# An attention-and-experts kernel: f's lead over q, k and v given up, and the last chunk's gate cut into thirds

## The chip, the cores and the metric

The kernel runs on one core of a Trainium2 chip. The metric is device time in microseconds; the median of 3 runs before the change is 465.24 us (465.19 to 465.57). The profile and trace below come from one profiled execution of the same kernel, with a span of 463.4 us and a mean granted TensorE clock of 0.97.

Five engines work in their own order and wait for each other through semaphores: TensorE (PE in the profile; its weight loads are PEld), VectorE (DVE), ScalarE (ACT), GpSimd (POOL) and SyncE (SP), whose queue issues the loads.

## The reference

Two blocks follow one another. The first is a gated linear recurrence over 768 steps for 4 batches and 8 heads of 48 columns; the second sends each of the resulting 3072 rows to one of 8 experts of equal capacity (384 rows).

```python
# attention block: q, k, v, f_logit are (4, 8, 768, 48)
f = 1.0 / (1.0 + np.exp(-f_logit))
for t in range(S):
    state = f[:, :, t, :, None] * state + np.einsum('bhd,bhe->bhde', k[:, :, t], v[:, :, t])
    y[:, :, t] = np.einsum('bhd,bhde->bhe', q[:, :, t], state)
# bridge: x is (3072, 384)
# experts block: w_gate (384, 8), w1 (8, 384, 1024), w2 (8, 1024, 384)
logits = x @ w_gate
order = np.argsort(-logits.flatten())      # best first; each row taken once, 384 rows an expert
...                                        # assigned[row] = expert
for e in range(E):
    mask = assigned == e
    out[mask] = np.maximum(x[mask] @ w1[e], 0.0) @ w2[e]
```

## The kernel before

The recurrence is worked in 24 chunks of 128 time steps (6 along the sequence, 4 batches; chunk i is batch i % 4). Each chunk passes through small functions. A step of the loop calls each of them for a chunk that depends on the function's stage: stage s in step n works on chunk n - s. Each engine takes its instructions in the order in which the functions are called.

```python
def load(G, names):
    b, c = G["b"], G["c"]
    for nm in names:                       # 192 KB each, pieces of 192 bytes
        ...
        nc.sync.dma_start(out=t[:], in_=src[b, :, C * c:C * c + C, :].rearrange("h t d -> t h d"))

def clamp(G):                              # GpSimd, f alone
    nc.gpsimd.tensor_scalar(out=f[:], in0=f[:], scalar1=3.0e38, scalar2=-40.0, ...)
def decays(G):                             # ScalarE, f alone: g = ln(1 + exp(-f))
    nc.scalar.activation(out=f[:], in_=f[:], func=AF.Exp, bias=0.0, scale=-1.0)
    nc.scalar.activation(out=g[:, :, 0:DH], in_=f[:], func=AF.Ln, bias=1.0, scale=1.0)
def split(G):                              # from chunk 2 on: g as high + low
    nc.vector.tensor_scalar(out=upper[:], ...)
    nc.gpsimd.tensor_tensor(out=low[:], in0=g[:, :, 0:DH], in1=upper[:].bitcast(FP32), op=ALU.subtract)
def sums(G):                               # TensorE: running sums L of g (two matmuls, high and low)
    ...
def factors(G):                            # VectorE dl from L, ScalarE eq = exp(-dl), ek = exp(dl)
    ...
def halves(G):                             # TensorE: sums of g over each half chunk ("ends")
    ...
def gated_q(G): ...                        # VectorE:  qg = q * eq
def gated_k(G): ...                        # GpSimd:   kg = k * ek  (VectorE for chunk 0)
def span(G): ...                           # VectorE spans, GpSimd and ScalarE gl: decay of the whole chunk
def columns(G, nm, t):                     # TensorE: transposes T of qg or kg
    if G["i"] in (1, 2):
        idle_turns(4, ps("nothing", "sum"))
    ...
def decayed(G): ...                        # GpSimd: R = state * gl
def added(G): ...                          # TensorE dS = kg' v ("states")
def scores(G): ...                         # TensorE A = kT' qT, VectorE copy_predicated into am
def values(G): ...                         # TensorE Y = am' v
def queries(G): ...                        # TensorE Y += qT' R; ScalarE copies Y to x; x stored to xd

def transposed(G):
    X = ps("X")
    for d in range(DC):                    # DC = 3
        nc.tensor.transpose(out=X[:, 128 * d:128 * d + 128],
                            in_=G["x"][:, 128 * d:128 * d + 128], identity=ident[:])
    G["X"] = X
def x_copy(G, work=work):
    G["xT"] = work.tile([128, DC, 128], FP32, name="xT", tag="xT")
    nc.vector.tensor_copy(out=G["xT"][:].rearrange("p c t -> p (c t)"), in_=G["X"][:, 0:D])
def gate(G):
    X = G["X"]
    for d in range(DC):
        for j in range(2):
            half = slice(HC * j, HC * j + HC)
            nc.tensor.matmul(out=X[half, D:D + E], lhsT=G["xT"][:, d, half], rhs=wg[:, d, :], ...)
def counts_so_far(G):
    if G["i"] == len(chunks) - 1:
        begun[3]()                         # counted(): 20 matmuls, then need = wanted - counts
```

`idle_turns` are matmuls of constants whose result nobody reads; they keep TensorE occupied. f has 3 buffers, q and k 4 each, v 7. The loop, with the orders of a step while the pipe fills, when it is full, and at the end:

```python
FIRST = ((decayed, 2), (q_columns, 2), (k_columns, 2), (transposed, 5), (sums, 0))
FILLING = (FIRST + ((x_copy, 5), (gated_q, 1), (gated_k, 1), (factors, 0), (k_copy, 2),
                    (added, 2), (values, 4), (halves, 0), (gate, 5),
                    (new_state, 2), (decays, -1), (span, 0), (to_logits, 5),
                    (split, -1), (beside, 0), (clamp, -2), (queries, 4), (split_high, -1),
                    (scores, 3)))
FULL = ((decayed, 2), (decays, -1), (transposed, 5), (sums, 0), (added, 2), (x_copy, 5),
        (gated_q, 1), (gated_k, 1), (factors, 0), (split, -1), (split_high, -1), (k_copy, 3),
        (halves, 0), (new_state, 2), (values, 4), (span, 0), (gate, 5), (to_logits, 5),
        (q_columns, 2), (k_columns, 2), (k_last, 2), (beside, 0), (clamp, -2), (queries, 4),
        (scores, 3))
LAST = ((scores, 3),) + FIRST + ((x_copy, 5), (k_copy, 2), (values, 4), (queries, 4),
                                 (counts_so_far, 5), (gate, 5), (to_logits, 5), (beside, 5))

def attention(first, last):
    for step in range(first, last):
        for ahead, names in (AHEAD + 1, "f"), (AHEAD, "qkv"):      # AHEAD = 2
            if AHEAD <= step + ahead < len(chunks) and (ahead == AHEAD or step >= 0):
                load(chunks[step + ahead], names)
        for part, stage in (FILLING if step < STAGES else           # STAGES = 6
                            FULL if step < len(chunks) + 2 else LAST):
            if 0 <= step - stage < len(chunks):
                part(chunks[step - stage])
            ...

for n, names in (0, "f"), (1, "f"), (0, "qk"), (2, "f"), (0, "v"), (1, "qkv"):
    load(chunks[n], names)
nc.sync.dma_start(out=wg[:], ...)
...
idle_turns(19, ps("nothing", "sum"))
clamp(chunks[0])
attention(-1, 2)
idle_turns(12, ps("nothing", "sum"))
attention(2, 3)
nc.vector.memset(a_bufs[2][:], 0.0)        # the third score buffer
```

After the last step come, on VectorE, the best logit of each row of the last column of chunks, its choice, its key, the steps that it reaches (`above`) and the pick; then TensorE counts rows per expert, the first of a search with which the routing begins. The experts' matmuls follow and fill the rest of the span.

Of the kernel before, what the change touches and what calls it, by code (L numbers as in the profile page):

```python
# [26 lines left out]
def kernel(  # L27
# [132 lines left out]
    def load(G, names):  # L160
        b, c = G["b"], G["c"]
        for nm in names:
            src = {"f": f_logit, "q": q, "k": k, "v": v}[nm]
# [35 lines left out]
    def sums(G):  # L199
        g = g_bufs[G["i"] % NB]  # L200
        G["L"] = L = ps("L")
# [136 lines left out]
    def queries(G):  # L338
# [12 lines left out]
        for par in range(2):  # L351
            copy = nc.vector.tensor_copy if par and G["i"] == len(chunks) - 1 else nc.scalar.copy
            copy(out=x[:].rearrange("t (a r d) -> t r a d", r=2, d=DH)[:, par],
                 in_=Y[par][:, 0:HP * DH].rearrange("t (a d) -> t a d", d=DH))
        row = S * b + C * c
        nc.scalar.dma_start(out=xd[row:row + C, :], in_=x[:])

    def transposed(G):
        X = ps("X")
        for d in range(DC):  # L360
            nc.tensor.transpose(out=X[:, 128 * d:128 * d + 128],
                                in_=G["x"][:, 128 * d:128 * d + 128], identity=ident[:])
        G["X"] = X

    def x_copy(G, work=work):
        G["xT"] = work.tile([128, DC, 128], FP32, name="xT", tag="xT")
        nc.vector.tensor_copy(out=G["xT"][:].rearrange("p c t -> p (c t)"), in_=G["X"][:, 0:D])

    def gate(G):
        X = G["X"]  # L370
        for d in range(DC):
            for j in range(2):
                half = slice(HC * j, HC * j + HC)
                nc.tensor.matmul(out=X[half, D:D + E], lhsT=G["xT"][:, d, half], rhs=wg[:, d, :],
                                 start=(d == 0), stop=(d == DC - 1))

    def counts_so_far(G):
        if G["i"] == len(chunks) - 1:
            begun[3]()

    def to_logits(G, to=None):
        if to is None:
            to = logits[:, G["b"] * NCH + G["c"]]
        nc.vector.tensor_copy(out=to, in_=G["X"][:, D:D + E])
# [5 lines left out]
    def beside(G):  # L390
# [9 lines left out]
    FIRST = ((decayed, 2), (q_columns, 2), (k_columns, 2), (transposed, 5), (sums, 0))  # L400
    FILLING = (FIRST + ((x_copy, 5), (gated_q, 1), (gated_k, 1), (factors, 0), (k_copy, 2),
                        (added, 2), (values, 4), (halves, 0), (gate, 5),
                        (new_state, 2), (decays, -1), (span, 0), (to_logits, 5),
                        (split, -1), (beside, 0), (clamp, -2), (queries, 4), (split_high, -1),
                        (scores, 3)))
    FULL = ((decayed, 2), (decays, -1), (transposed, 5), (sums, 0), (added, 2), (x_copy, 5),
            (gated_q, 1), (gated_k, 1), (factors, 0), (split, -1), (split_high, -1), (k_copy, 3),
            (halves, 0), (new_state, 2), (values, 4), (span, 0), (gate, 5), (to_logits, 5),
            (q_columns, 2), (k_columns, 2), (k_last, 2), (beside, 0), (clamp, -2), (queries, 4),
# [923 lines left out]
```

## Time and profile before

| what | value | how to read it |
|---|---|---|
| median time | 465.24 us | 3 runs |
| span of the profiled execution | 463.4 us | 11905 instructions |
| PE busy | 439.1 us (95%) | TensorE; its ends are modelled |
| DVE, ACT, POOL busy | 257.5, 138.8, 131.3 us | 56, 30 and 28% of the span |
| f, q, k, v loads | 24 each of 192 KB | 4.2 to 4.5 us from issue to landing |
| DMA in attention | 160 to 205 GB/s | in the slices up to 116 us |
| experts' matmuls, H and O | 132.6 + 67.0 + 66.7 us | 496 and 491 ns each |
| idle turns, all | 20.2 us | 71 of them |

The page divides the span into 40 slices of 11.6 us. Attention takes about the first fourteen of them: its last logits are copied at 159.54 us. The rest is routing and the experts. The chain that ended last tells little here, since its list holds only the last few microseconds of the queues; the stages have to be read from the timeline instead.

### The profile page before, as it was taken

What the parts mean: (1) busy time and instruction counts of PE and PEld (TensorE: products, weight loads), DVE (VectorE), ACT (ScalarE), POOL (GpSimd) and SP (SyncE); (2) the same over time, 40 slices, a digit from 0 to 9 for tenths busy, and PEclk for the clock granted to TensorE, in tenths of its full rate; (3) what the DMA queues carried; (4) which work ended last, traced back from release to release, by engine and by line L of the source; (5) the groups of instructions that cost most, each with busy time, mean ns of one, the idle gap of its engine ahead of it and who ended that gap; (6) DMA issues with size and microseconds to landing.
All of it is one profiled execution on the core that took longest, in us unless ns stands there. A gap on an engine that the chain in (4) does not pass through costs nothing. (4 is left out here: it accounts for less than half of the span.)

```text
span 463.4 us, 11905 instructions
## 1 busy us (share of the span) xinstructions
PE 439.1 (95%) x4890; PEld 294.6 (64%) x4890; DVE 257.5 (56%) x878; ACT 138.8 (30%) x322; POOL 131.3 (28%) x189
## 2 busy tenths in 40 slices
PE   6898999999998759999999999999999999999994
PEld 3687888888887635565555555555555565556552
DVE  6468777777886677647737737737737737000000
ACT  3556655666552001212212212212212212212210
POOL 2546545555551012023013013013013015201001
PEclk9989999999999857999999999999999999999998
DMA  9999998878511109073072072072072076500001
GB/s 160 180 205 193 202 192 173 177 172 179 124 38 37 54 2 306 18 261 97 18 274 85 18 272 87 18 272 85 19 272 86 17 272 227 202 16 37 0 18 38
DMA packets 118399, 59.11 MB, mean 128 GB/s; under 512 B 101664, under 2 KB 112960, under 8 KB 118336
## 3 DMA queue, kind: packets, MB, share of 16 engines
q1 hardware_dynamic: 111760, 44.06, 38.3%
q0 software_dynamic: 3072, 9.44, 6.2%
q10 hardware_dynamic: 3504, 4.77, 3.0%
q8 instruction: 40, 0.66, 0.6%
q14 instruction: 23, 0.19, 0.1%
HBM read 48.77 MB, written 9.49 MB: 126 GB/s over the span
## 5 line engine op out<-in xcount | busy, mean ns | idle before, releaser
L1054 PE MATMUL H<-xeT,w 128*128 128x384 f32 x384 | 132.6, 496 | 0.1
L1054 PEld LDWEIGHTS H<-xeT,w 128*128 128x128 f32 x384 | 69.1, 190 | 45.7 <-issue 4.0
L1066 PE MATMUL O<-w,hT 128*128 128x384 f32 x192 | 67.0, 491 | 0.0
L1066 PE MATMUL last_O<-w,hT 128*128 128x384 f32 x192 | 66.7, 491 | 0.0
L1058 ACT ACTIVATE hT<-H 128x384 f32<-128x384 f32 x64 | 31.4, 491 | 101.3 <-PE H L1054 85.3
L1066 PEld LDWEIGHTS last_O<-w,hT 128*128 128x128 f32 x192 | 35.1, 190 | 22.8 <-issue 1.9
L1066 PEld LDWEIGHTS O<-w,hT 128*128 128x128 f32 x192 | 34.9, 190 | 21.5 <-issue 1.3
L322 DVE COPY_PREDICATED am<-mask,A 128x512 f32<-128x512 int32 x48 | 32.3, 728 | 26.0 <-PE A L317 26.0
L1071 POOL DMA_INDIRECT out_dram<-o,token x21 | 21.2, 1012 | 83.6 <-ACT o L1070 83.3
L191 POOL TENSOR_TENSOR low<-g,upper 128x384 fp32r<-128x384 f32 x22 | 23.7, 1078 | 54.8 <-DVE upper L189 29.8
L971 POOL TENSOR_TENSOR block<-past 128x72 f32<-128x72 f32 x8 | 2.4, 300 | 111.6 <-DVE at L551 100.3
L1046 ACT COPY xeT<-Xe 128x384 f32<-128x384 f32 x24 | 11.4, 479 | 58.1 <-PE Xe L1043 57.9
L332 PE MATMUL Y<-v,am 128*64 128x48 f32 x768 | 27.5, 223 | 1.3 <-DVE am L322 1.3
L317 PE MATMUL A<-qT,kT 48*64 48x128 f32 x768 | 26.8, 276 | 0.2 <-issue 0.2
L332 PEld LDWEIGHTS Y<-v,am 128*64 128x64 f32 x768 | 24.7, 138 | 2.4 <-DVE am L322 2.0
L1013 POOL DMA_INDIRECT xe<-xd,token x21 | 21.4, 1021 | 10.9 <-DVE full L548 4.4
L218 ACT ACTIVATE eq<-dl 128x384 f32<-128x384 f32 x24 | 12.5, 523 | 38.1 <-DVE dl L216 38.1
L241 POOL TENSOR_TENSOR kg<-k,ek 128x384 f32<-128x384 f32 x23 | 23.1, 1005 | 0.0
L317 PEld LDWEIGHTS A<-qT,kT 48*64 48x64 f32 x768 | 21.4, 135 | 1.0 <-issue 0.9
L127 PE MATMUL nothing<-idle,ones 128*128 128x384 bf16 x71 | 20.2, 427 | 1.6 <-DVE ones L132 1.5
L1070 ACT COPY o<-O 128x384 f32<-128x384 f32 x12 | 5.8, 479 | 40.7 <-PE O L1066 40.7
L1070 ACT COPY o<-last_O 128x384 f32<-128x384 f32 x11 | 5.3, 479 | 40.5 <-PE last_O L1066 40.5
(223 smaller groups left out, 659.7 us busy)
## 6 DMA issues: line engine op xcount, KB each, us to landing
w<-in_moe_w_dram SPq DMA_DIRECT2D x16, 1536.0 KB, 7.3
f<-in_f_logit_dram SPq DMA_DIRECT2D x24, 192.0 KB, 4.5
q<-in_q_dram SPq DMA_DIRECT2D x24, 192.0 KB, 4.2
k<-in_k_dram SPq DMA_DIRECT2D x24, 192.0 KB, 4.4
v<-in_v_dram SPq DMA_DIRECT2D x24, 192.0 KB, 4.4
xd<-x ACTq DMA_DIRECT2D x24, 192.0 KB, 2.7
xe<-xd,token POOLq DMA_INDIRECT x21, 3.1
out_dram<-o,token POOLq DMA_INDIRECT x21, 2.6
```

Of the source, the lines that this page charges most:

```text
L127: nc.tensor.matmul(out=nothing[:, 0:CAP], lhsT=ones[:], rhs=idle[:], start=True, stop=True)
L191: nc.gpsimd.tensor_tensor(out=low[:], in0=g[:, :, 0:DH], in1=upper[:].bitcast(FP32), op=ALU.subtract)
L218: nc.scalar.activation(out=G["eq"][:], in_=dl[:], func=AF.Exp, bias=0.0, scale=-1.0)
L241: engine.tensor_tensor(out=G["kg"][:, :, 0:DH], in0=G["k"][:], in1=G["ek"][:], op=ALU.mult)
L317: nc.tensor.matmul(out=A[par][HC * j:HC * j + HC, 128 * hp:128 * hp + 128], lhsT=G["kT"][rows, hp, HC * j:HC * j + HC], rhs=G["qT"][rows, ...
L322: nc.vector.copy_predicated(am[:, par], mask[:].unsqueeze(1).to_broadcast((128, HP, 128)), A[par][:].rearrange("s (a t) -> s a t", t=128))
L332: nc.tensor.matmul(out=Y[par][HC * j:HC * j + HC, DH * hp:DH * hp + DH], lhsT=G["am"][:, par, hp, HC * j:HC * j + HC], rhs=G["v"][:, 2 * h ...
L1013: nc.gpsimd.indirect_dma_start(out=xe[:], out_offset=None, in_=xd[:, :], in_offset=bass.IndirectOffsetOnAxis(ap=token[:, i:i + 1], axis=0))
L1054: nc.tensor.matmul(out=L["H"][:, 0:CAP], lhsT=L["w1"][:, d, 128 * ft:128 * ft + 128], rhs=xT[:, d, :], start=(d == 0), stop=(d == DC - 1))
L1058: nc.scalar.activation(out=hT[:, ft, :], in_=L["H"][:, 0:CAP], func=AF.Relu)
L1066: nc.tensor.matmul(out=L["O"][:, 0:D], lhsT=hT[:, ft, 128 * i:128 * i + 128], rhs=L["w2"][:, ft, :], start=(ft == 0), stop=(ft == FC - 1))
L1071: nc.gpsimd.indirect_dma_start(out=outs[next(tiles)][:, :], out_offset=bass.IndirectOffsetOnAxis(ap=L["token"][:, i:i + 1], axis=0), in_=o ...
```

## The change

Two things are changed together.

First, f loses its lead. Before, f of chunk n+3 is loaded in the same step as q, k and v of chunk n+2, and all that needs f alone (clamp, decays, split, sums, halves, factors, span) runs one stage earlier than it would have to; a step -1 precedes the others. After, the four tiles of a chunk are loaded one after the other, f first, and those functions have moved one stage later. Gating of q and k stays at stage 1 and now follows the factors of the same chunk in the same step. Three idle turns are put before the sums of chunk 5, where the order of a step changes. The aim is a simpler order with one step fewer.

Second, the last chunk's path to its logits is cut into thirds: each of the three transposes gets a bank of its own, is copied by itself (the middle one by ScalarE), and the gate's matmuls start on the first third; the gate has its own bank. The counts of the other columns, which stood between transposes and gate on TensorE, are put behind the gate, and the subtraction that uses them behind the last picks. The aim is a shorter path from the last x to its logits.

```diff
-    def load(G, names):
+    def load(G):
         b, c = G["b"], G["c"]
-        for nm in names:
-            src = {"f": f_logit, "q": q, "k": k, "v": v}[nm]
+        for nm, src in (("f", f_logit), ("q", q), ("k", k), ("v", v)):
@@
     def sums(G):
         g = g_bufs[G["i"] % NB]
+        if G["i"] == STAGES - 1:
+            idle_turns(3, ps("nothing", "sum"))
@@
     def transposed(G):
-        X = ps("X")
+        G["X"] = X = [ps("X") for _ in range(DC)] if last(G) else [ps("X")] * DC
         for d in range(DC):
-            nc.tensor.transpose(out=X[:, 128 * d:128 * d + 128],
+            nc.tensor.transpose(out=X[d][:, 128 * d:128 * d + 128],
                                 in_=G["x"][:, 128 * d:128 * d + 128], identity=ident[:])
-        G["X"] = X
 
     def x_copy(G, work=work):
-        G["xT"] = work.tile([128, DC, 128], FP32, name="xT", tag="xT")
-        nc.vector.tensor_copy(out=G["xT"][:].rearrange("p c t -> p (c t)"), in_=G["X"][:, 0:D])
+        if last(G):
+            G["xT"] = [work.tile([128, 128], FP32, name="xTd", tag="xTd", bufs=DC)
+                       for _ in range(DC)]
+            for d, t in enumerate(G["xT"]):
+                copy = nc.scalar.copy if d == 1 else nc.vector.tensor_copy
+                copy(out=t[:], in_=G["X"][d][:, 128 * d:128 * d + 128])
+        else:
+            ...                            # as before
 
     def gate(G):
-        X = G["X"]
+        G["lg"] = lg = ps("lg") if last(G) else G["X"][0]
         ...
     def counts_so_far(G):
-        if G["i"] == len(chunks) - 1:
-            begun[3]()
+        if last(G):
+            G["need"] = begun[3]()
@@
-    FIRST = ((decayed, 2), (q_columns, 2), (k_columns, 2), (transposed, 5), (sums, 0))
-    ...
+    FIRST = ((decayed, 2), (q_columns, 2), (k_columns, 2), (transposed, 5), (sums, 1))
+    FILLING = (FIRST + ((x_copy, 5), (factors, 1), (k_copy, 2),
+                        (added, 2), (values, 4), (halves, 1), (gate, 5), (gated_q, 1),
+                        (new_state, 2), (decays, 0), (gated_k, 1), (span, 1), (to_logits, 5),
+                        (split, 0), (beside, 0), (clamp, -1), (queries, 4), (split_high, 0),
+                        (scores, 3)))
+    FULL = ((decayed, 2), (decays, 0), (transposed, 5), (sums, 1), (added, 2), (x_copy, 5),
+            (factors, 1), (split, 0), (split_high, 0), (k_copy, 3), (halves, 1), (new_state, 2),
+            (values, 4), (span, 1), (gate, 5), (gated_q, 1), (gated_k, 1), (to_logits, 5),
+            (q_columns, 2), (k_columns, 2), (k_last, 2), (beside, 0), (clamp, -1), (queries, 4),
+            (scores, 3))
     LAST = ((scores, 3),) + FIRST + ((x_copy, 5), (k_copy, 2), (values, 4), (queries, 4),
-                                     (counts_so_far, 5), (gate, 5), (to_logits, 5),
+                                     (gate, 5), (to_logits, 5), (counts_so_far, 5),
                                      (beside, 5))
@@
-            for ahead, names in (AHEAD + 1, "f"), (AHEAD, "qkv"):
-                if AHEAD <= step + ahead < len(chunks) and (ahead == AHEAD or step >= 0):
-                    load(chunks[step + ahead], names)
+            if step + AHEAD < len(chunks):
+                load(chunks[step + AHEAD])
@@
-                    for _ in range(min(len(small), 1 if step >= len(chunks) + 2 else 2)):
+                    for _ in range(min(len(small), 2)):
@@
-    for n, names in (0, "f"), (1, "f"), (0, "qk"), (2, "f"), (0, "v"), (1, "qkv"):
-        load(chunks[n], names)
+    for G in chunks[0:AHEAD]:
+        load(G)
@@
-    attention(-1, 2)
+    attention(0, 2)
@@
-            tt(need[0:NTH, :], wanted[0:NTH, :], r[0:NTH, 0:E], ALU.subtract)
+            return lambda: tt(need[0:NTH, :], wanted[0:NTH, :], r[0:NTH, 0:E], ALU.subtract)
@@
         if n == 2:
             at_steps(NCH - 1, NCH)
+    chunks[-1]["need"]()
```

## The prediction

> **What bounds the kernel now.** I began with the page's second part, the busy tenths in 40 slices of 11.6 us.
>
> ```profile
> PE   6898999999998759999999999999999999999994
> PEclk9989999999999857999999999999999999999998
> DMA  9999998878511109073072072072072076500001
> ```
>
> TensorE is the bound. Gaps show only at the start (slices 0 to 3) and at the hand-over from attention to routing (slices 12 to 15, 139 to 185 us), the two places that the change touches. DMA is near full for seven slices, so the new loading order might starve something. The answer by stages gives the steady part (columns: TensorE, weight loads, VectorE, ScalarE, GpSimd busy, clock, DMA share, GB/s):
>
> ```profile
> 84.00:96.00 12.00, 12.00 (x317) 10.52 (x318) 8.65 (x22) 7.64 (x20) 6.34 (x11) 1.00 0.82 179
> ```
>
> No gap: a step is 5.68 us (value matmuls start at 85.34 and 91.02). Both orders put the same TensorE work into such a step, so it should keep its length.
>
> The timeline of the first 31 us (start, duration, what, idle time and who ended it) shows what paces the filling:
>
> ```profile
> 7.56 0.56 DVE L216 TENSOR_SCALAR dl<-L 128x384 f32<-128x384 f32 x1 [1.34 <-PE L L209]
> 8.02 0.51 POOL L173 TENSOR_SCALAR f<-f 128x384 f32<-128x384 f32 x1 [2.66 <-DMA f<-in_f_logit_dram]
> 9.00 0.51 ACT L178 ACTIVATE f<-f 128x384 f32<-128x384 f32 x1
> 10.11 0.91 PE L209 MATMUL L<-g,wcum 128*128 128x384 f32 x2 [2.02 <-ACT g L179]
> 13.48 0.60 PE L259 MATMUL T<-ident,qg 128*128 128x128 f32 x4
> 18.78 2.25 POOL L191 TENSOR_TENSOR low<-g,upper 128x384 fp32r<-128x384 f32 x1 [2.06 <-DVE upper L189]
> 21.09 0.45 PE L205 MATMUL L<-low,wcum_r 128*128 128x384 f32 x1 [1.34 <-POOL low L191]
> 24.05 1.46 PE L127 MATMUL nothing<-idle,ones 128*128 128x384 bf16 x4
> 30.78 0.66 PE L259 MATMUL T<-ident,qg 128*128 128x128 f32 x4
> ```
>
> The sums L of consecutive chunks form a chain that goes round four engines: L, clamp dl, the two exponentials, exp and ln of the next f, its split, the next L. L starts at 6.7, 10.1, 14.5, 19.3 (second half 21.1), 27.3. Loads end only three waits of it, 5.3 us in total in the list of waits, all early. So the filling is a latency chain, one turn per step, and it matters how many turns pass before the q and k transposes get going. Before, a step n holds L of chunk n and the transposes of chunk n-2; step 5 starts at 30.78.
>
> The end of attention, from the same timeline:
>
> ```profile
> 157.81 0.52 PE L361 MATMUL X<-ident,x 128*128 128x128 f32 x3 [0.20 <-DVE x L353]
> 158.36 0.56 DVE L367 COPY xT<-X 128x384 f32<-128x384 f32 x1
> 158.97 0.52 PE L374 MATMUL X<-wg,xT 128*64 128x8 f32 x12
> 159.54 0.17 DVE L384 COPY logits<-X 128x8 f32<-128x8 f32 x1 [0.43 <-PE X L374]
> 160.67 0.25 PE L767 MATMUL cnt<-choice,above 128*16 128x8 bf16 x4 [1.18 <-DVE above L544]
> ```
>
> Transposes, one copy of 384 columns, gate, logits: strictly one after the other. The 20 matmuls of the counts (158.27 to 158.92) hide under the copy.
>
> [...] asked by single microseconds, the clock is half from 22.9 to 26.3 (3.4 us), and the four idle turns at 24.05 last 1.46 us, against 0.82 at full clock. [...] low (18.78) takes 2.25 us while VectorE clears a score buffer for 0.91 us and multiplies q after it; alone it takes 1.01. [...] Here f of chunk 2, issued fifth, is ready at 8.02.
>
> **The change part by part.**
>
> *Start.* It takes f's lead away: step n now holds L of chunk n-1 and still the transposes of chunk n-2. It also drops step -1, which held only one exp and ln. So the transposes come one turn of the chain earlier, if the loads allow it.
>
> Loads first. f1 moves from second to fifth place. By the place of f2 before, it is ready at 8.02; its exp waited for ScalarE until 9.00 anyway. f2 comes after nine large tiles of 0.197 MB. Bytes by single microseconds reach 1.77 MB at 11.1; f2 before had its 0.98 MB at 6.9 and was ready 1.2 later, so 12.3, at most 13.1 if SyncE's issue is late. f3, 13th, by the same count 16.6; f4 20.8; f5 24.9.
>
> Now the turns, with durations of the rows above. L(0) as before: 6.7. Twelve idle turns (2.1) until 10.2. Transposes of chunk 0 at 10.2 instead of 13.5 (qg ends at 9.27). L(1) then 11.05, 0.9 later than before; dl 12.0, exponentials until 13.55, exp and ln of f2 until 14.6, split 14.95. The clearing of the third score buffer now falls on low(2): about 1.0 + 0.9, done at 16.9. L(2) ends at 17.4; dl(2) 17.4 to 18.0, exponentials until 19.0, f3 until 20.05, low(3) done at 21.5. TensorE meanwhile: transposes of chunk 1 until 15.7, L(2), states and chunk ends until 18.4, scores(0) until 19.5, idle turns and transposes of chunk 2 until 22.2, L(3) 22.2 to 22.9, states 0.5, values(0) 1.1, ends 0.5, scores(1) 1.1: 26.0. Step 5 thus starts at 26.0 against 30.78: 4.8 us earlier, with TensorE saturated from here. Step 6 then waits for x as before (0.64 and 0.37 idle there); the three new idle turns (0.6) lie in that wait, worth 0.1 of cost. Left: 4.7.
>
> *Owed back.* At equal step numbers the new order is one L and its chunk ends behind. They land in step 24, where TensorE idled for the predicated copies (0.35 and 0.28 us before the values at 141.43 and 142.04). L 0.76 plus ends 0.5 minus the wait filled and the overlap: values end about 0.35 later. Net 4.35.
>
> *End.* First transpose done at about 158.1. Thirds: VectorE 158.1 to 158.4, ScalarE 158.2 to 158.5 (its DMA issue ends at 158.08), VectorE 158.36 to 158.64. Only the last third of the gate follows; logits at about 159.0 instead of 159.54. The counts run behind the gate, 159.0 to 159.65, before the next counts at 160.1. The subtraction `need` (0.15) slips between pick and fills, where VectorE waited anyway, at up to 0.1. Gain 0.4.
>
> Sum at full clock: 4.35 + 0.4 = 4.75, giving 460.5.
>
> **The rivals.** First, the clock. Before lost some 1.6 us to the half-clock window at 22.9 (3.4 us of work at half speed). My schedule has none. [...] Should it trip, the eight idle turns, transposes and L(3) run at half speed: about 2.3 us, giving 462.8. I think this as likely as not. Second, loads become the bound: f8 has to be there at 42 and by 200 GB/s comes at 41. Steps 6 to 9 are tight; a slip of one tile each would cost 1 to 2 us. Against it: between 48 and 84 us the DMA share is 0.83 to 0.95 with TensorE without a gap, and buffer counts are the same. Third, f's lead was useful in the steady part, and without it TensorE waits for low or gated k. In the step around 104 us gated k would follow gl (done at 105.0) and end at 106.0; its user, the states, is at 107.33, a slack of 1.3. low has most of a step. A wait of 0.3 us on 18 steps would cost 5 and cancel everything. Fourth, the gain is swallowed later: routing waits for the w tiles. Their loads are issued by the routing itself, so they move along.
>
> **Range and chances.** The mean of 460.5 and 462.8 is 461.65; I say 461.6. Low end: everything at full clock and no issue delays, 459.8. High end: half clock and a slip of one load, 463.9. A gain of 2% would need 455.9, twice my best case; a loss of 2% needs 474.5, which only the third rival, at twice the size I gave, could reach.
>
> **What would show it.** Right: transposes of chunk 0 near 10.2; the exp of f1 still near 9.0; step 5 (transposes of chunk 3) near 26; a step of 5.68 in mid-course; step 24 longer than 5.3; logits some 1.2 us after the last transposes begin, instead of 1.7. Wrong: GpSimd waiting on loads of f beyond the first four chunks, a gap on TensorE before L or the states in the middle, or chunk 0's transposes not before 13.

## The result

The changed kernel takes **459.61 us** (median of 4 runs, 458.42 to 460.65), the kernel before 465.4 us beside it (4 runs, 465.19 to 465.87). The ratio is 0.9873, 95% interval 0.9848 to 0.9899: within 2%, and 5.8 us faster where 3.6 was predicted. The range began at 459.8. Measured again (`same_again` below) the same kernel gave 459.87.

The page of the kernel after, second part, the same rows as were shown of before (busy tenths in 40 slices, here of 11.5 us):

```profile
PE   8999999999999669999999999999999999999994
...
PEclk9999999999999758999999999999999999999998
DMA  9999989878511117082082082082082087400001
```

TensorE is at 9 from the second slice on, where the kernel before began with 6, 8, 9, 8, and its dip of the clock in the third slice is gone: the granted clock is full (1.00 from 5.1 to 155.3 us) until the hand-over to the routing. DMA is as full until slice 7 as it was. The answer by stages for the stretch that the prediction used (TensorE, weight loads, VectorE, ScalarE, GpSimd busy, clock, DMA share, GB/s) reads

```profile
84.00:96.00 12.00, 11.70 (x300) 10.12 (x297) 8.31 (x28) 7.12 (x18) 6.77 (x10) 1.00 0.86 188
```

Before it was 12.00 of 12.00 with 317 matmuls. TensorE now has small gaps in the middle of attention.

The timeline of the filling of the kernel after (start, duration, engine, line, operation, idle time and who ended it):

```profile
6.36 0.81 PE L211 MATMUL L<-g,wcum 128*128 128x384 f32 x2
...
9.30 0.52 ACT L177 ACTIVATE f<-f 128x384 f32<-128x384 f32 x1 [0.58 <-POOL f L172]
...
9.62 0.60 PE L261 MATMUL T<-ident,qg 128*128 128x128 f32 x4
...
12.78 0.68 POOL L172 TENSOR_SCALAR f<-f 128x384 f32<-128x384 f32 x1 [3.51 <-DMA f<-in_f_logit_dram]
...
15.04 1.01 POOL L190 TENSOR_TENSOR low<-g,upper 128x384 fp32r<-128x384 f32 x1 [0.62 <-DVE upper L188]
15.13 0.91 DVE L456 MEMSET am<- 128x1024 f32 x1 [0.16 <-DVE upper L188]
...
17.45 0.51 POOL L172 TENSOR_SCALAR f<-f 128x384 f32<-128x384 f32 x1 [1.40 <-DMA f<-in_f_logit_dram]
...
20.65 0.42 PE L207 MATMUL L<-high,wcum_r 128*128 128x384 f32 x1
...
24.17 0.66 PE L261 MATMUL T<-ident,qg 128*128 128x128 f32 x4
```

The reader sees the transposes of chunk 0 at 9.62 (13.48 before), and those of chunk 3, with which step 5 begins, at 24.17 (30.78 before; 26.0 predicted). Low at 15.04 takes 1.01 us although the clearing of the score buffer runs beside it from end to end.

How the lead over the kernel before fares from there is best read from the start of the value matmuls of each chunk, before minus after (us). The second column is the same kernel measured again, the third a kernel told of below that leaves most loads out:

```
chunk     after   same_again   few_loads
  0        6.61      6.55         6.29
  2        7.26      7.20         6.94
  5        7.18      6.70         6.98
  9        7.72      7.48         8.02
 11        7.50      6.24         8.03
 13        6.59      6.12         8.17
 15        5.37      6.11         8.11
 17        4.88      5.98         8.32
 23        4.50      5.27         7.29
```

So the filling gave 6.6 to 7.7 us, two to three of which came off again by chunk 23. The end of attention in the same timeline of the kernel after:

```profile
153.30 0.52 PE L367 MATMUL X<-ident,x 128*128 128x128 f32 x3 [0.20 <-DVE x L355]
...
153.75 0.27 ACT L376 COPY xTd<-X 128x128 f32<-128x128 f32 x1 [0.73 <-PE X L367]
...
154.56 0.17 DVE L397 COPY logits<-lg 128x8 f32<-128x8 f32 x1 [0.41 <-PE lg L387]
...
155.41 0.23 DVE L555 TENSOR_TENSOR above<-over,steps 128x64 bf16<-128x64 f32 x1
...
155.88 0.14 DVE L555 TENSOR_TENSOR need<-wanted,counted 16x8 f32<-16x8 f32 x1
...
156.07 0.24 PE L778 MATMUL cnt<-choice,above 128*16 128x8 bf16 x4 [0.98 <-DVE need L555]
...
156.40 0.15 DVE L555 TENSOR_TENSOR fills<-cnt,need 16x8 f32<-16x8 f32 x1 [0.39 <-PE cnt L778]
```

From the last transposes to logits it takes 1.26 us (1.73 before), as predicted. But the first count of the routing starts 0.66 us behind `above` instead of 0.28, released by `need`. From the last transposes to `fills` it is 3.10 us, against 3.22 before (157.81 to 161.03): of 0.47 us gained, 0.12 is left.

### The profile page after: what moved, and what is told of

It reads as the page before. It is cut to its first block, busy times and chain, and to the rows that moved or that the text cites. A ratio compares the mean times of both kernels' runs of the same rounds, so it can differ in the third digit from the quotient of the medians.

```text
span 458.9 us, 11904 instructions
## 1 busy us (share of the span) xinstructions
PE 437.8 (95%) x4893; PEld 294.2 (64%) x4893; DVE 265.9 (58%) x879; ACT 139.3 (30%) x323; POOL 136.0 (30%) x189
## 5 line engine op out<-in xcount | busy, mean ns | idle before, releaser
L190 POOL TENSOR_TENSOR low<-g,upper 128x384 fp32r<-128x384 f32 x22 | 22.3, 1012 | 44.9 <-DVE upper L188 44.1
L1081 ACT COPY o<-O 128x384 f32<-128x384 f32 x12 | 5.7, 478 | 40.8 <-PE O L1077 40.8
L237 DVE TENSOR_TENSOR qg<-q,eq 128x384 f32<-128x384 f32 x24 | 17.5, 727 | 0.6 <-ACT eq L220 0.6
```

What stands on the lines that cost most here:

```text
L237: nc.vector.tensor_tensor(out=G["qg"][:, :, 0:DH], in0=G["q"][:], in1=G["eq"][:], op=ALU.mult)
```

## The experiments

All are timed beside runs of the kernel before on the same chip, and ratios are to it. The kernel before gave medians of 466.03, 465.3, 465.76 and 465.52 us in the four groups.

### One part alone, and f's loads put back

`thirds_only` is the kernel before with the cut into thirds, the counts behind the gate, the later `need` and the line on the small pieces of a step (`min(len(small), 2)`). `stages_only` is the other part alone. `same_again` is the kernel after. `f_loads_ahead` keeps the new stages of after, but loads f one chunk ahead as before did:

```diff
-    def load(G):
-        for nm, src in (("f", f_logit), ("q", q), ("k", k), ("v", v)):
+    def load(G, names="fqkv"):
+        for nm in names:
...
-                          bufs={"f": 3, "q": 4, "k": 4, "v": 7}[nm])
+                          bufs={"f": 4, "q": 4, "k": 4, "v": 7}[nm])
...
-            if step + AHEAD < len(chunks):
-                load(chunks[step + AHEAD])
+            for ahead, names in (AHEAD + 1, "f"), (AHEAD, "qkv"):
+                if step + ahead < len(chunks):
+                    load(chunks[step + ahead], names)
...
-    for G in chunks[0:AHEAD]:
-        load(G)
+    for n, names in (0, "f"), (1, "f"), (0, "qk"), (2, "f"), (0, "v"), (1, "qkv"):
+        load(chunks[n], names)
```

> The kernel before with the second part of the change alone (last chunk by thirds, counts behind the gate, subtraction behind the picks). Theory 1: the logits of the last chunk come 0.5 us earlier after the last transposes, but the first count of the routing waits for the deferred subtraction, so only 0.1 to 0.2 us is left: 465.2 +- 0.3. Rival (the end brings what was predicted): 464.9 or less by 0.4 to 0.5.

> The kernel before with the first part alone (f loses its lead; last chunk as before). Theory 1: nearly all of the gain, 5.5 us, so 459.8 (458.5 to 461). Rival (the two parts share it): 462 or more.

> The changed kernel once more, to see how far its executions spread. Theory 1 (the slow steps between 83 and 131 us are stalls of TensorE that hang on the moment, not on the order): values of chunk 5 again some 7.2 us ahead of before, the slow steps at other places or fewer, the time between 458 and 461. Rival (the new order itself makes steps slow): the same steps are slow again, 6.1 to 6.9 us from chunk 11 to 15, and the time is 459.6 or more.

> The changed kernel with its stages, but with f loaded one chunk ahead of q, k and v again (a fourth buffer for f). In the filling of the changed kernel eight clamps in a row wait for f, 14.1 us in total. Theory 1 (these waits pace the chain of sums): the clamps of chunks 1 to 5 wait no more, step 5 starts 0.5 to 1.5 us earlier than 24.2, time 458.5. Rival (the chain is paced by its own latency, and the waits are idle time of an engine that has nothing else to do): step 5 within 0.4 us of 24.2, time as of the changed kernel within its spread.

Measured: `thirds_only` 465.9 us, ratio 0.9997 (0.9971 to 1.0023); `stages_only` 460.77, 0.9873 (0.9839 to 0.9906); `same_again` 459.87, 0.9854 (0.9798 to 0.991); `f_loads_ahead` 459.97, 0.9859 (0.9804 to 0.9915). The stages make the difference; the thirds give nothing that these runs can measure. In `same_again` the slow steps lie elsewhere: 6.70 us behind chunk 9 and at most 6.0 from chunk 12 to 15, where the profiled run of the kernel after has 6.12 to 6.87. So they do not hang on the order alone.

Loading f ahead starts step 5 at 23.35, 0.8 us earlier, as its first theory had it: the waits for f did pace the filling. The values of chunks 3 to 7 come another 1.4 to 2.0 us earlier than in `same_again` (lead 8.4 to 8.7), but the lead is 6.5 at chunk 10 and 5.8 at chunk 23 (5.3 in `same_again`), and the time is the same, against the theory's 458.5. Most of what that run gains in the filling does not last.

### Late stores

In the traces the store of x is issued late on ScalarE. From the timeline of the kernel after around one such store (ACTq and SPq are the issues of DMAs):

```profile
69.38 0.54 ACT L355 COPY x<-Y 128x192 f32<-128x192 f32 x2
...
70.68 0.34 ACTq L358 DMA_DIRECT2D xd<-x  x1
...
71.06 0.52 ACT L177 ACTIVATE f<-f 128x384 f32<-128x384 f32 x1 [1.14 <-POOL R L286]
71.39 0.80 SPq L166 DMA_DIRECT2D f<-in_f_logit_dram  x1
```

The copies of x are done at 69.92, the store leaves at 70.68, and the exponential of the next f stands behind it. In the traces of both kernels every load and store of attention carries one of eight semaphores, nearly in turn, and none leaves before the earlier transfer with the same one has landed (0.07 us behind that landing at the least in the kernel after, 1.1 us in the kernel before). For the store that is usually a load of one or two steps ago. Beside each store of the kernel after, the earlier load on its semaphore (from the trace, us; 0.03 behind the copies is a store on time):

```
store issued   late by   earlier transfer   issued   landed
   58.10         0.03           k           52.63    57.91
   64.47         0.73           v           58.48    64.40
   70.68         0.76           f           65.07    70.60
   77.05         1.45           f           71.39    76.97
   82.00         0.32           f           76.75    81.92
   87.59         0.41           f           81.72    87.51
   93.88         0.03           f           87.17    93.34
```

Each late store leaves 0.07 to 0.08 us after that load has landed. In the kernel before the wait is there too, but the loads are in time (at 77.68 us, for example, the load in question had landed at 74.86), and no store but the last is late. In `same_again` seven stores from 53 to 89 us are late, by up to 2.06 us, in `f_loads_ahead` eight, by up to 2.34.

The late stores can't be the whole loss. Behind 87.59 us no store of the kernel after is late, yet its lead falls from 6.9 at chunk 12 (89.76 us) to 4.9 at chunk 17. Four runs tell whether the wait is part of it:

```diff
# store_later: behind the two exponentials and the high part of the next step
-        row = S * b + C * c
-        nc.scalar.dma_start(out=xd[row:row + C, :], in_=x[:])
+        G["unstored"] = 1
+        if not 2 <= G["i"] < len(chunks) - 3:
+            stored(G)                      # the same dma_start, once
...
-            (factors, 1), (split, 0), (split_high, 0), (k_copy, 3), (halves, 1), ...
+            (factors, 1), (split, 0), (split_high, 0), (stored, 5), (k_copy, 3), (halves, 1), ...
# need_early
         if n == 2:
             at_steps(NCH - 1, NCH)
-    chunks[-1]["need"]()
+            chunks[-1]["need"]()
# store_before: the edit of store_later in the kernel before
# all_three: store_later, need_early and f_loads_ahead together
```

> The kernel after, but ScalarE issues the store of x of a chunk in the next step, behind the two exponentials and the rounding of the high part, instead of at once behind the copies of x (chunks 2 to 20). Loop theory: between 53 and 90 us the store waits for the landing of an earlier load (it was issued 0.06 to 0.08 us after that landing each time it was late), the exp and ln of the next f stand behind it on ScalarE, and they free the buffer of f into which the next load goes, so that a step cannot be shorter than that load. With the store out of this loop the delays of 0.3 to 2.1 us no longer sit ahead of exp; the lead of the value matmuls over the kernel before stays above 7 us from chunk 7 to chunk 13 instead of falling to 6.1 to 6.6 there, and the time falls by 0.8 to 1.5 us, to 458.4 to 459.1. Load theory (the stream of loads is simply full until 90 us, and whoever waits for it only changes): GpSimd's waits for f grow instead, steps between 48 and 90 us stay at 6.0 to 6.3 us, and the time stays within 0.3 us of 459.8.

> The kernel after, but the subtraction need is issued directly behind the thirds' last counts instead of after the last step, so that the psum tile it reads is given back earlier. Theory: the first count of the routing waits 0.66 us behind the comparison above because VectorE does need ahead of it (0.28 us in the kernel before); with need earlier this falls to 0.3, and the time from logits to fills from 1.84 to about 1.5 us: 0.3 us less in all, 459.5. Rival: need only moves in front of another VectorE operation on the path, and the time from logits to fills stays at 1.8.

> The kernel after with three edits: the store of x later (as in the run before the last), need earlier, and f loaded one chunk ahead of q, k and v with a fourth buffer for f. Loop theory: f loaded ahead brought values of chunk 3 to 7 another 0.9 to 1.3 us earlier, and lost it all again to late stores; with the store out of the loop most of it stays: 457.0 to 458.0. Load theory: the stream of loads sets the pace until 90 us in every one of these kernels, and the time is the same as with the later store alone, less 0.3 for need.

> The kernel before with the later store alone. There the store was never late (0.03 us at every chunk but the last), so the loop theory expects no difference: 465.4 plus or minus 0.4. If the place of the store on ScalarE mattered in itself, the time would change here too.

Measured: `store_later` 459.14 us (458.61 to 459.63), ratio 0.9859 (0.9823 to 0.9895); `store_before` 465.14, 0.9993 (0.997 to 1.0017). In `store_later` the store goes 2.9 us behind the copies where it waits for nothing, but between 57 and 75 us it is 3.7 to 4.9 behind them: it still waits there, for loads of q, k and v that take about 5 us, and now the end of the step stands behind it. The lead falls to 6.5 by chunk 9. 459.14 is at the edge of what I had named for the loop theory and 0.5 to 0.7 below the two medians of the kernel after, inside their spread. The loop through exp and the buffer of f is thus not shown to be the cause.

`need_early`: 458.96 us, ratio 0.9856 (0.9813 to 0.9899). The times alone don't show so small a step, but the timeline does. From `need_early`:

```profile
153.64 0.17 DVE L397 COPY logits<-lg 128x8 f32<-128x8 f32 x1 [0.41 <-PE lg L387]
...
154.49 0.23 DVE L555 TENSOR_TENSOR above<-over,steps 128x64 bf16<-128x64 f32 x1
154.63 0.14 DVE L555 TENSOR_TENSOR need<-wanted,counted 16x8 f32<-16x8 f32 x1
...
154.83 0.24 PE L778 MATMUL cnt<-choice,above 128*16 128x8 bf16 x4 [0.66 <-DVE need L555]
...
155.18 0.15 DVE L555 TENSOR_TENSOR fills<-cnt,need 16x8 f32<-16x8 f32 x1
```

From logits to `fills` it takes 1.54 us instead of 1.84, the 0.3 expected. The subtraction reads `counted`, which matmuls have left in a psum tile, and only when it is done does the tile pool of attention end and the first count of the routing begin. Issued late, it stood in front of the very path that it had been moved out of.

`all_three`: 458.65 us (457.66 to 459.75), ratio 0.9852 (0.9814 to 0.989), lead 7.1 at chunk 9 and 6.4 at chunk 23. It is the lowest median of a kernel that does all the work, and lies where the load theory has it (459.14 less 0.3), not at the 457 to 458 of the loop. The last of the four groups has `both_plus`, the same without the later store:

> The kernel after with need earlier and f loaded one chunk ahead with a fourth buffer, the store of x where it was. Load theory (the place of the store on ScalarE hardly matters, the stream of loads does): the same as with the later store added, 458.65 plus or minus 0.4. If the later store was worth something: 459.3 or more.

Measured: 459.03 us (457.96 to 460.1), ratio 0.9863 (0.9827 to 0.9899). It began 8.4 to 9.2 us ahead at chunks 2 to 7 and was 6.3 ahead at chunk 23, about as far as `all_three`. The later store shows no worth. Either combination is faster than the kernel before; that one of them beats the kernel after by the 0.6 to 1.0 us of the medians is not shown, as the intervals overlap. Only the 0.3 of `need` is plain in a trace.

### Are the loads the limit?

```diff
# few_loads (in the kernel after), few_before (in the kernel before)
+            if nm != "f" and G["i"] > 8:
+                G[nm] = chunks[8][nm]
+                continue
             t = work.tile([128, H, DH], FP32, name=nm, tag=nm,
# store_gpsimd: store_later, but for chunks 2 to 20
-            nc.scalar.dma_start(out=xd[row:row + C, :], in_=G["x"][:])
+            nc.gpsimd.dma_start(out=xd[row:row + C, :], in_=G["x"][:])
```

`few_loads` and `few_before` leave out the loads of q, k and v of chunks 9 to 23, which then use the tiles of chunk 8; the amount of work on the engines is the same.

> The kernel after, leaving out the loads of q, k and v behind chunk 8: the later chunks use those of chunk 8, so three quarters of the load traffic from about 42 us on are gone and the values are other ones. Load theory in either form: no late store and no lost microsecond behind chunk 8; the lead is 7.2 or more at chunk 13 and about 6.8 at the end, the time about 457.5 to 458.2. If the losses in the middle come from the new order of the work itself, or from stalls of TensorE that have nothing to do with loads, the lead still falls to 6.5 or less by chunk 13.

> The kernel before, leaving out the loads of q, k and v behind chunk 8 (the later chunks use those of chunk 8, so the values are other ones). The same cut made the kernel after 1.7 to 2.0 us faster than without it. If the limit by loads is something that the earlier filling has brought on, the kernel before gains next to nothing by it: 465.0 to 465.5, lead at chunk 13 below 0.4. If fewer loads help any order of the work (by less traffic on SBUF, say), it gains 1.5 us or more too: 463.8 or less.

> The kernel after, but x of chunks 2 to 20 is stored by GpSimd (behind the subtraction low of the next step) and not by ScalarE, so that the store shares its semaphore with no load. If the wait of the store for a load is what costs the middle, ScalarE never stands behind it: lead of the value matmuls at chunk 13 stays at 7.0 or more (6.1 to 6.6 in the kernel after), and the time is 458.5 to 459.0. If the stream of loads itself is the limit between 48 and 80 us, the lead falls by the same 0.7 to 1.2 us between chunks 7 and 11 as before, with GpSimd or ScalarE waiting for f, q or k, and the time stays at 459.6 to 460. The issue may cost GpSimd itself about a microsecond a step, which would show in gl and kg coming late.

Measured: `few_loads` 457.91 us (457.71 to 458.26), ratio 0.9827 (0.9789 to 0.9866); `few_before` 465.68, ratio 1.0002 (0.9977 to 1.0028). Without most loads the kernel after is 1.7 to 2.0 us faster by the medians (the intervals of the ratios overlap), and the kernel before is not faster; its interval leaves room for a gain of 1.1 us at most. The answer by stages of the kernel after:

```profile
60.00:72.00 12.00, 11.71 (x316) 10.37 (x316) 8.76 (x26) 6.92 (x18) 6.77 (x10) 1.00 0.91 195
...
96.00:108.00 12.00, 11.27 (x281) 9.86 (x279) 8.57 (x23) 7.25 (x18) 6.77 (x10) 1.00 0.89 191
```

and of `few_loads`:

```profile
60.00:72.00 12.00, 12.00 (x336) 10.78 (x332) 9.28 (x26) 7.04 (x18) 6.79 (x10) 1.00 0.28 69
...
96.00:108.00 12.00, 12.00 (x313) 10.69 (x312) 9.79 (x26) 7.45 (x19) 7.26 (x12) 1.00 0.28 70
```

With a DMA share of 0.3 instead of 0.9 TensorE has no gap from 48 to 120 us, no store is late, and the lead of 8.0 at chunk 9 is still 8.3 at chunk 17 (the table above). This trace decides: the loads take back what the filling gains. That they do so only where the kernel starts early enough is what the two times of `few_before` and the kernel before suggest. In the trace of `few_before`, which has half clock at 10.4 to 17.2 and 24.0 to 30.8 us and is 4.2 us behind at chunk 0, the distance to the kernel before stays the same from chunk 9 to chunk 23 within 0.2 us. `few_loads` takes away the traffic of q, k and v and also SyncE's waits for their buffers to come free; no run adds buffers, so which of the two limits is not shown.

`store_gpsimd` took 467.59 us, ratio 1.0033 (1.0011 to 1.0054), slower than either expectation had it. The store shares no semaphore with loads there, but its issue occupies GpSimd for 0.6 us, and between 117 and 136 us TensorE waits 0.4 us for x and 0.3 to 0.4 us for the predicated copies in every step. Another 3.8 us are lost behind chunk 23 (lead 0.56 there, span 3.2 us longer), unexplained. It has put other costs in place of the wait and tells nothing of the wait.

### The start: the clearing, and the clock

The prediction took low(3) of the kernel before, 2.25 us long, for the effect of the clearing of the score buffer. Two runs move that clearing in the kernel before, one into the constants, one behind the gated q:

```diff
# clear_early
         nc.vector.memset(a_bufs[1][:], 0.0)
+        nc.vector.memset(a_bufs[2][:], 0.0)
...
-    nc.vector.memset(a_bufs[2][:], 0.0)
# clear_behind_q (and the same line taken out)
         nc.vector.tensor_tensor(out=G["qg"][:, :, 0:DH], in0=G["q"][:], in1=G["eq"][:], op=ALU.mult)
+        if G["i"] == 2:
+            nc.vector.memset(a_bufs[2][:], 0.0)
```

> The kernel before with the third score buffer cleared among the constants, and no longer beside low of chunk 3. If that clearing made low(3) 2.25 us long (as I read it in the prediction), low(3) takes 1.0 to 1.5 us now. If the gated q (two operands from SBUF) did it, low still takes 1.5 or more, longer the more of it lies beside qg. If it is neither, 2.25 us stay.

> The kernel before with the clearing of the third score buffer issued behind the gated q of chunk 2 instead of ahead of it; low of chunk 3 still lies beside it. Low took 2.25 us with the clearing ahead of qg, 1.25 with qg alone beside it, and 1.01 in the kernel after with the clearing alone. [...] low takes 1.2 to 1.4 us now. If the clearing itself slows GpSimd, it takes 2.0 or more.

The timeline of the kernel before, VectorE beside the low of 2.25 us (18.78 to 21.03):

```profile
18.86 0.91 DVE L445 MEMSET am<- 128x1024 f32 x1 [0.16 <-DVE upper L189]
...
19.69 0.49 DVE L235 TENSOR_TENSOR qg<-q,eq 128x384 f32<-128x384 f32 x1
```

of `clear_early`:

```profile
18.57 0.55 DVE L236 TENSOR_TENSOR qg<-q,eq 128x384 f32<-128x384 f32 x1
...
18.74 1.25 POOL L192 TENSOR_TENSOR low<-g,upper 128x384 fp32r<-128x384 f32 x1 [2.06 <-DVE upper L190]
```

and of `clear_behind_q`:

```profile
21.10 0.55 DVE L235 TENSOR_TENSOR qg<-q,eq 128x384 f32<-128x384 f32 x1
...
21.26 1.25 POOL L191 TENSOR_TENSOR low<-g,upper 128x384 fp32r<-128x384 f32 x1 [3.44 <-DVE upper L189]
...
21.81 0.91 DVE L238 MEMSET am<- 128x1024 f32 x1 [0.16 <-issue]
```

(The two took 466.31 and 467.75 us, one time each, with half clock later in the filling.) By the expectation of `clear_early` its 1.25 us spoke for the clearing as the cause; `clear_behind_q`, with the clearing beside low again and 1.25 us all the same, refutes that. The same clearing beside the same low: 1.25 us when it is issued behind qg, 2.25 or 2.26 when it is issued ahead of it (six traces), 1.01 (kernel after) when no qg is near. So the clearing by itself cost low nothing, and qg by itself 0.24 us (`clear_early`). My reading of the 2.25 us was wrong. Why low lost 1.0 us more with the clearing ahead of qg no trace shows.

The clock was to be tested with six idle turns where TensorE stood still for 1.34 us in L(3) of the kernel before, alone and with the loads cut as above:

```diff
# warm_before; warm_few = this and the cut of few_loads
             for n, term in enumerate(G["terms"]):
+                if n and G["i"] == 3:
+                    idle_turns(6, ps("nothing", "sum"))
```

> The kernel before with six idle turns of TensorE between the high and the low matmul of L(3), where it stood still for 1.34 us ahead of the half-clock window of 22.9 to 26.3 us. If that gap brought the window on, the window is gone, the transposes of chunk 3 begin 1.5 us earlier (29.3), and the time falls by about 1.5 us to 463.7: this much of the step from before to after is then the clock's. Rival: the window comes whatever stands there; no change, 465.3.

> The kernel before with the six idle turns in L(3) (no half clock at 22.9) and without the loads of q, k and v behind chunk 8. The idle turns alone brought the values of chunk 0 1.7 us forward, of chunk 9 2.2, and of chunk 23 only 1.0, with stores of x late by 0.8 to 2.0 us between 47 and 66. If loads took that back, the lead now stays at 2.0 or more to the end and the time is 463.3 or less; if something else did, it is 1.0 at the end as with the idle turns alone, 464.4 to 465.4.

Measured: `warm_before` 465.41 us (462.73 to 466.64), ratio 0.9984 (0.9964 to 1.0003); `warm_few` 464.53 (462.4 to 466.47), ratio 0.996 (0.993 to 0.9989). The time of `warm_before` is its rival's. In its profiled run there was no half clock at 22.9 and the transposes of chunk 3 began at 29.07, as expected, but there was a window at 11.0 to 14.4, ahead of the idle turns (19.49), which thus did not bring it. It was 1.7 us ahead at chunk 0, 2.2 at chunk 9 and 1.0 at chunk 23, with four stores late by 0.8 to 2.0 us. In the profiled run of `warm_few` the half clock came at 35.9 to 42.7 and took the lead of 2.0 at chunk 0 away, so what I expected of its end can't be read; from chunk 9 to chunk 23 it lost nothing. What the idle turns did to the half clock these two runs don't show. The granted clock of all profiled runs up to 150 us says more (`few_before`, whose profiled execution took 471.23 us against its median of 465.68, is left out):

```
order of before   half clock at (us)              order of after    half clock
before            22.9-26.3                       after             none
thirds_only       22.1-25.6, 39.2-42.6            same_again        none
store_before      10.8-17.6, 24.4-31.2            stages_only       none
clear_early       36.5-46.7                       f_loads_ahead     none
warm_before       11.0-14.4                       store_later       none
warm_few          35.9-42.7                       need_early        none
clear_behind_q    10.0-16.9, 37.4-47.6            all_three         none
                                                  store_gpsimd      none
                                                  few_loads         none
                                                  both_plus         none
```

All windows are one, two or three times 3.4 us long; in that of the kernel before the granted clock is 0.50. Seven of seven profiled executions with the old order have at least one, none of ten with the new order has any. The mean granted clocks of the timed executions point the same way, less sharply: 0.959 to 0.976 in the kernel before, 0.973 to 0.980 in the new order (`store_gpsimd`, 0.957 to 0.978, and one execution of `stages_only` at 479.13 us apart). But three of the 22 of `warm_before` have 0.979 or 0.980. That leaves no room for a window in the filling, as the hand-over to the routing alone takes at least 17 us of half clock in every trace. A window of 3.4 us costs an estimated 1.7 us at most (3.4 at half speed). Why the windows fall where they do no run shows.

## Why the prediction was wrong

The direction, the part that does it, the steady step and a change of less than 2% were right; the size was not, 3.6 us for 5.8. Two steps failed on the low side. The filling was worked out too slow: 4.7 us of lead, where 7.7 was measured at chunk 9. And half clock in the new filling was given even odds, 1.15 us of the estimate, where no trace of the new order has it. Two failed on the other side: the loads, where I saw room, took 2.2 us back in the profiled run, and at the end of attention 1.05 us is owed back, not 0.35. They partly cancel, so it is in part luck that the time came as near as 0.2 us to the range.

**The start.** "Transposes of chunk 0 at 10.2": 9.62. "Exp of f1 still near 9.0": 9.30. f2 "12.3, at most 13.1": 12.78. f3, f4 and f5 came at 17.45, 21.82 and 26.55, each 0.85 to 1.65 us later than I had them. That a tile's place in the order of issue sets its arrival, on which these times rest, agrees with both traces: each load of attention lands behind the one issued before it, the first five of the kernel after at 3.78, 5.16, 6.21, 7.25 and 8.33 us. One turn of the chain fewer was the right mechanism. The step that failed is "the clearing of the third score buffer now falls on low(2): about 1.0 + 0.9, done at 16.9". Low was done at 16.05. Then "idle turns and transposes of chunk 2 until 22.2" counted the eight idle turns and the eight transposes at 2.7 us behind the scores; they took 2.1, as they overlap (18.55 to 20.65). The rest of the step was 0.3 shorter. In all step 5 began 1.8 us before the 26.0 of the prediction, although f came later than I had it; with f ahead it is 2.65 (23.35).

**Step 6.** "Step 6 then waits for x as before (0.64 and 0.37 idle there)": in its place stands one wait of 0.29 us at 29.59. With two stalls of the kernel before (steps of 6.27 and 6.04 instead of 5.68 us behind the values of chunks 6 and 8) the lead grew to 7.7 by chunk 9, where 4.7 was predicted.

**The clock.** The first rival, half clock in the new filling "as likely as not", moved the estimate by 1.15 us in the wrong direction. No profiled run of the new order showed it; in the profiled runs the half clock goes with the old order. I had one trace of before to go by, with its window at 22.9, while in the seven traces windows begin anywhere from 10.0 to 39.2; the even odds were my estimate, and what brings a window on is not shown. Without this rival my own sum stood at 460.5, in spite of the terms above.

**The loads.** The second rival, "steps 6 to 9 are tight; a slip of one tile each would cost 1 to 2 us", was right in size, 1.7 to 2.0 us by `few_loads`, and later than I had it: between 50 and 120 us. I weighed against it that DMA had a share of 0.83 to 0.95 "with TensorE without a gap". The step that failed is this reading. The answer by stages of the kernel before has gaps there:

```profile
60.00:72.00 12.00, 11.82 (x307) 10.36 (x307) 8.49 (x25) 7.02 (x18) 6.19 (x11) 1.00 0.83 176
72.00:84.00 12.00, 11.85 (x310) 10.61 (x310) 8.48 (x24) 7.24 (x19) 6.33 (x11) 1.00 0.91 191
```

With 11.94 from 48 to 60, TensorE lacks 0.39 us in that stretch, where the two stalls of above lie; only 84 to 96 is without a gap. The DMA share was a sign of loads just in time, not of room: starting 7 us earlier needs the same bytes 7 us earlier. One of my signs of being wrong came too: GpSimd waited for f in each of the first eight chunks, 14.1 us in all, and not in the first four only. That f8 "by 200 GB/s comes at 41" does not follow from the count used for f2 to f5, which gives 37.2 (4.1 a chunk); it was issued at 36.1 and landed at 40.8. How the loads slow TensorE stays open: moving the store made no clear difference, and much of the loss comes where no store is late.

**The third rival**, that f's lead was of use in the steady part, fell: in `few_loads` the values of chunks 9 to 13 follow each other by 5.67 or 5.68 us, as before, and f loaded ahead does not change the time. (Twice its size would have given 471.3, not the 474.5 that I named.) The fourth, a gain swallowed by the routing, fell as well: what attention was ahead at chunk 23 stayed to the end (4.50 there, 4.6 in the time of that run).

**Owed back.** 0.35 was predicted for step 24. From chunk 16 to chunk 23 the lead falls by 1.03 to 1.08 us in all nine traces of the new order but `store_gpsimd`, with most loads and without, so this is the order's own term and three times what I had. The last 0.2 of it comes behind chunk 19, where I had put the whole; 0.8 comes ahead of it. In that stretch VectorE has no pause: it is busy 12.00 of 12.00 us from 117 to 129 in `few_loads` and 11.50 of 11.50 from 121 to 132.5 in the kernel after, against 11.63 of 13.00 from 125 to 138 before, and TensorE waits for its predicated copies (0.2 to 0.3 us). Why VectorE is busier there no run tests.

**The end.** Logits came 1.26 us after the last transposes, as predicted. The 0.28 to 0.3 us for the copy of a third were my estimate; it took 0.29 us on VectorE and 0.27 on ScalarE. The step that failed is "`need` slips between pick and fills, where VectorE waited anyway, at up to 0.1": it cost 0.3, as the psum tile that it reads had to be free before the first count. Of the 0.4 of gain 0.1 is left.

The balance by the trace of the slowest run of the kernel after: 7.72 us at chunk 9, less 2.15 by chunk 16, less 1.07 in the last chunks, plus 0.1 at the end, 4.6; the three other runs are 1.0 to 2.2 us faster than this one.

## What to carry to other kernels

A kernel that is filled faster must be fed earlier: where DMA is near full from the start, as here (8 or 9 tenths in each of the first eight slices), an earlier start is worth only what the loads can follow, and a run with most loads left out measures the difference in one go. Before a limit is ruled out by the stages, look at each stretch that the argument names, and not at the cleanest one alone. If a latency chain can be shortened by a stage, look at the granted clock of both orders over several runs before giving the half clock even odds; it may be the old order that pays for it, as here in seven traces of seven. An operation that is postponed because nobody waits for its result may still hold a buffer that somebody waits for, here for 0.3 us.

## What I had not expected of the hardware

- A VectorE clearing of 0.91 us and a GpSimd subtraction of 1.01 us ran side by side without loss (kernel after), but the subtraction took 2.25 or 2.26 us where the VectorE product qg was issued behind the clearing (six traces), and 1.25 where the product went first (`clear_behind_q`).
- A store issued by ScalarE waited for a load that has nothing to do with it, where both carried the same one of eight semaphores: up to 2.34 us (`f_loads_ahead`), each time ended within 0.1 us of that load's landing where the trace has it.
- The half clock in the filling lies anywhere between 10 and 48 us in the seven traces of one order of the work and is absent in the ten of the other, with nearly the same work in both.
